# Token mixing in batches 2 to 4: one column half for each pair of TensorE column groups, and another order of the later steps

## The chip, the cores and the metric

The kernel runs on one core of a Trainium2 chip. Its time is the device time of one execution in microseconds, lower is better; several executions are taken, and their median counts. A core has five engines that run their own instruction lists side by side and wait for each other through semaphores: TensorE (PE in the profile; its weight loads are PEld), VectorE (DVE), ScalarE (ACT), GpSimd (POOL) and SyncE (SP), the last two mostly for issuing transfers here. TensorE is an array of 128 rows and 128 columns that can be cut into blocks, such as four of 64x64 or four column groups of 128x32. It writes to PSUM, eight banks of 512 float32 numbers in each of 128 partitions; VectorE and ScalarE move results to SBUF.

## What is computed

Four batches, 768 tokens, 8 heads of 48 (384 columns together). First a delta-rule recurrence for each head, then a mixer on its output:

```python
y[:, :, t] = np.einsum('bhd,bhde->bhe', q[:, :, t], state)
v_old = np.einsum('bhde,bhd->bhe', state, kt)
state = state + bt[:, :, :, None] * np.einsum('bhd,bhe->bhde', kt, vt - v_old)
...
xt = x.transpose(0, 2, 1)
h = xt @ U @ V
u = x + h.transpose(0, 2, 1)
ch = np.maximum(u @ w_ch1, 0.0) @ w_ch2
return (u + ch).astype(np.float32)
```

U is 768 x 32 and V is 32 x 768. The token mixing of one batch is therefore two small products: the first, U transposed times x, is a 32 x 384 matrix with a sum over all 768 tokens; the second, V transposed times that, is added to x.

## The kernel before

All is float32. The recurrence is worked in chunks of 64 tokens, twelve a batch, from Gram matrices (`products`, L461), triangular solves (VectorE's pairs at L530 and L532, `joins`, L591 to L640) and a chain of small matmuls from chunk to chunk (`recur`, L687 to L790: `outputs`, states, corrections). Its output lands in the tile X, one half of the tile for each of two batches in turn. The mixer of a batch starts when all twelve chunks stand in X, while the recurrence of the next batch goes on beside it.

The mixer of batch b goes over three tiles of 256 tokens (i = 0, 1, 2). For each, `front(b, i)` mixes the tokens and turns the result (L1198, or L229 and L233) so that channels lie on partitions; `wide(b, i)` does the two channel layers (`channels`, L1264, and in a crossed form on 64x64 blocks at L221; `narrow`, L1358 and also L221; the sum into X at L1304). The first tile of batch 1, the last tile of batch 3 and all of batch 4 go through forms of their own (L1088 to L1143, L1041, L997). The code counts batches from 0: b = 1, 2, 3 are batches 2, 3 and 4.

The lines that the change touches are the head of `front`:

- First product, `token_product` (L1060): X holds tokens in six blocks of 128 on the partitions. For each of the four column groups g of the array (128 rows x 32 columns) it multiplies a 128 x 32 block of U with a 128 x 384 block of X. Groups 0 and 2 go over the even token blocks, groups 1 and 3 over the odd ones, so groups 0 and 2 have one sum and groups 1 and 3 the other, each twice. Twelve matmuls of 384 columns a batch, into one PSUM bank.
- L1172 copies the result, 128 partitions x 384 columns, to the SBUF tile `tt`. Partitions 0 to 63 and 64 to 127 hold the same two partial sums.
- Second product (L1186), in each of the three tiles: the array is cut into four 64x64 blocks. A block's 64 rows are the even and the odd partial sum, which the product adds up; V lies on the partitions four times (`v_sb`). Block row m makes the m-th 128 tokens of the tile, block column q one half of these. Four matmuls of 384 columns; block row m writes to bank m of a pair.
- L1189 adds both banks to X, 128 x 768 numbers.

Nothing chooses an order at run time. Each part (`front`, `channels`, `recur`, a load and so on) is a generator that yields whenever it wants to put an instruction or a small group on an engine. `ORDER`, a written-out list of 2719 numbers, says whose turn it is; behind a point stands the PSUM bank pair, and a q chooses the crossed form of a step. An engine runs its own steps in the order of this list, and semaphores hold it where data or a buffer is not ready. Numbers are given to parts as they begin, so one number can mean another part when the list changes.

Of the kernel before, what the change touches and what calls it, by code (L numbers as in the profile page):

```python
# [11 lines left out]
ALU = mybir.AluOpType  # L12
# [11 lines left out]
def kernel(ctx: ExitStack, tc: tile.TileContext, q: bass.AP, k: bass.AP, v: bass.AP, beta: bass.AP, moe_U: bass.AP, moe_V: bass.AP, moe_w_ch1: bass.AP, moe_w_ch2: bass.AP, out: bass.AP):  # L24
# [59 lines left out]
    297 71 207 61 297 301 208 61 297 301 61 61 208 298.2 297 303 298 207 68 304q 208 298 70 71 304 44 207  # L84
# [6 lines left out]
    332 331 331 331 331 332.1 336 332 162 334.2 334 332 9.0 333 337q 334 9 206 328.2 9.0 337 9 9.0 337 328  # L91
    337 9 328 61 328 332 9.0 348.2 9 9.1 337 205 206 9 9.0 349 350.1 205 206 348 9 9.0 206 205 348 338q 348
    9 205 206 338 9.2 338 338 9 338 351.0 9.2 352 350 9 162 350 339q 350 9.2 339 9 351 339 9.1 80 89 90 89
# [3 lines left out]
    344q 353 9 353 364 9.2 353 344 353 85 360 9 365.1 344 9.2 360 344 360 9 78 78 364 9.0 344 9 78 364 9.2  # L97
    366.0 343 365 9 9.2 365 365 368 207 208 9 78 367 9.1 208 207 78 369.2 78 85 345q 207 208 208 207 345 85
# [3 lines left out]
    347 180 85 375 358 180.0 358 376 98 180 181.1 85 374.2 85 377q 98 181 104 377 388.0 104 85 377 85 375  # L102
# [6 lines left out]
    102 102 102 102 391 387 391 102 409 102 10.0 410 182q.2 10 102 10.0 394 411 10 394 182 102 102 411 102  # L109
    102 102 422.0 423 102 408.1 10.2 102 412q 10 102 10.2 102 422 412 10 422 102 10.2 422 102 424.0 10 412  # L110
    102 10.2 408 412 408 10 102 412 102 10.1 426.2 425 424 10 102 10.1 424 413q 102 424 10 102 10.0 102 413
# [7 lines left out]
    112 10 112 112 446.2 112 119 10.0 421 449 119 440 449 119 10 10.0 450 446 440 450 451q 446 10 446 119  # L119
    119 10.1 451 119 10 119 462.0 119 10.2 451 119 451 10 119 119 10.1 119 462 451 119 10 447.2 119 464 119  # L120
    10.1 119 112 452 10 119 119 447 447 452 119 119 119 463.1 465 10.2 119 453 119 462 462 119 119 10 453
    119 119 10.0 466 468.2 463 10 119 10.0 463 454q 463 119 10 467 10.1 119 454 211 212 10 119 10.0 454 468
    211 212 469.1 10 468 162 10.0 212 376 468 454 10 162 211 212 10.2 119 454 409 10 119 471.0 211 470 10.2
    119 469 119 455 119 119 119 455 119 10 119 456 119 472 119 469 119 469 456 119 119 119 10.2 119 473 119
    10 119 471 141 141 141 140 141 140 131 140 140 131 458q 471 132 471 132 183.1 474 467 119 119 131 458
    183 140 141 119 183.2 162 141 140 458 458 119 141 138 183 138 141 458 119 138 139 119 183q.0 119 140 139
# [4 lines left out]
    121 136 481.2 136 142 501 481 136 491 136 481 136 481 136 483 136 491 136 136 136 136 184q.0 136 136  # L131
# [1320 lines left out]
```

## Time and profile before

| | us |
|---|---|
| median of three runs | 573.75 |
| lowest, highest | 572.85, 576.26 |
| the profiled execution, its own time | 572.55 |
| span of its instructions on the core | 570.8 |
| mean granted TensorE clock over the span | 0.976 |
| first product, L1060, all four batches: passes, mean of one | 96, 0.490 |
| second product, L1186, all twelve tiles: passes, mean of one | 96, 0.500 |
| sum into X, L1189, all twelve tiles: count, mean of one | 12, 0.943 |

The span goes from the first instruction to the last; the profiled execution's own time has 1.75 us around it. A float32 matmul appears in the profile as two passes, each with a weight load of its own (PEld). Passes on different blocks of the array run at the same time, so the durations of passes cannot be added up; the chain of waits gives what a group of them costs from the start of one to the start of the next. The page divides the span into 40 slices of 14.3 us with the busy share of each engine in tenths.

### The profile page before, as it was taken

How to read it: one execution, taken by the hardware profiler on the slowest of the kernel's cores; microseconds unless marked ns; L12 is line 12 of the kernel's file. 1: busy time of each engine (PE TensorE's matmuls, PEld its weight loads, DVE VectorE, ACT ScalarE, POOL GpSimd, SP SyncE). 2: the span in 40 equal slices, each digit the busy share in tenths (PEclk: the TensorE clock that was granted, in tenths of full speed). 3: DMA queues.
4: the chain of work that ended last, by engine and by line, in shares of the span. 5: the costliest groups of instructions: out<-in, count | busy, mean ns of one | idle time of the engine just before them, and what ended most of it. 6: DMA issues, size and time to landing. Idle time of an engine off the chain costs nothing.

```text
span 570.8 us, 24657 instructions
## 1 busy us (share of the span) xinstructions
PE 537.4 (94%) x10965; PEld 454.7 (80%) x10965; DVE 417.4 (73%) x1062; ACT 243.1 (43%) x525; POOL 130.0 (23%) x229
## 2 busy tenths in 40 slices
PE   4776989999999999999999999999999999999997
PEld 4675877669789688789879977988879888656997
DVE  5798976799897439999887889999653356656542
ACT  3786885452435453155236433632452341336100
POOL 8061064552201453131044133400000000000000
PEclk9997579999999999999999999999999999999999
DMA  9957766542200353250033233310000000100001
GB/s 144 184 124 224 229 179 138 117 100 53 72 3 17 78 126 85 53 103 3 3 78 83 66 86 64 81 27 2 17 4 2 31 2 1 41 2 0 15 14 57
DMA packets 70763, 38.67 MB, mean 68 GB/s; under 512 B 56768, under 2 KB 67776, under 8 KB 70656
## 3 DMA queue, kind: packets, MB, share of 16 engines
q1 hardware_dynamic: 62368, 25.87, 19.2%
q0 software_dynamic: 6688, 10.92, 8.2%
q8 instruction: 86, 1.41, 1.1%
q10 hardware_dynamic: 1600, 0.30, 0.3%
q14 instruction: 21, 0.17, 0.1%
HBM read 32.34 MB, written 4.72 MB: 65 GB/s over the span
## 4 chain that ended last, share of the span: by engine, by line
PE 82%; DVE 8%; ACT 3%; DMA 2%; SPq 2%; issue 2%; DVEq 0%; ACTq 0%
PE P L1358 26%; PE P L1264 14%; PE P L221 9%; PE P L997 7%; PE P L461 4%; PE P L1041 2%; PE P L1088 2%; PE P L780 2%; PE P L739 2%; PE P L752 2%; DMA slot<-in_k_dram 2%; PE P L1186 2%; PE P L687 1%; PE P L1060 1%; PE P L694 1%
## 5 line engine op out<-in xcount | busy, mean ns | idle before, releaser
L1264 PE MATMUL P<-ut,w_sb 128*128 128x256 f32 x360 | 83.1, 385 | 0.2 <-ACT hs L1234 0.2
L1358 PE MATMUL P<-w_sb,hs 128*128 128x192 f32 x456 | 80.4, 330 | 0.0
L1358 PEld LDWEIGHTS P<-w_sb,hs 128*128 128x128 f32 x456 | 73.9, 190 | 3.9 <-issue 1.8
L1264 PEld LDWEIGHTS P<-ut,w_sb 128*128 128x128 f32 x360 | 66.7, 190 | 9.6 <-ACT hs L1234 0.3
L532 DVE TENSOR_TENSOR xt<-xt,prod 128x112 f32<-128x112 f32 (+21 forms) x200 | 64.2, 321 | 5.1
L530 DVE TENSOR_TENSOR prod<-gs,xt 128x112 f32<-128x112 f32 (+21 forms) x200 | 63.7, 318 | 4.3
L1304 DVE TENSOR_TENSOR X<-X,P 128x192 f32<-128x192 f32 x85 | 29.4, 347 | 42.9 <-PE P L1358 42.1
L344 POOL DMA_DIRECT2D slot<-in_k_dram x48 | 27.7, 582 | 95.5 <-PE P L780 60.9
L1234 ACT ACTIVATE hs<-P 128x512 f32<-128x512 f32 x42 | 24.9, 598 | 56.2 <-PE P L1264 43.6
L677 ACT COPY X<-P 64x192 f32<-64x192 f32 x96 | 30.1, 313 | 35.1 <-PE P L694 30.4
L1358 PE MATMUL P<-w_sb,S 128*128 128x192 f32 x240 | 41.3, 328 | 0.0
L1358 PEld LDWEIGHTS P<-w_sb,S 128*128 128x128 f32 x240 | 39.0, 190 | 0.8 <-DVE X L1304 0.6
L221 PE MATMUL P<-ut,w_sb 64*64 64x256 f32 x576 | 39.0, 383 | 0.2
L653 ACT COPY slot<-zz 32x384 f32<-32x384 f32 x64 | 34.5, 540 | 8.4 <-DVE zz L536 5.4
L461 PE MATMUL P<-slot 48*64 48x64 f32 x1536 | 33.1, 243 | 4.0 <-ACT slot L437 3.0
L461 PEld LDWEIGHTS P<-slot 48*64 48x64 f32 x1536 | 30.3, 156 | 7.4 <-ACT slot L437 3.6
L344 POOL DMA_DIRECT2D slot<-in_q_dram x48 | 27.2, 572 | 32.7 <-DVE slot L450 14.4
L657 POOL MEMSET slot<- 32x384 f32 x32 | 13.8, 431 | 90.9 <-PE P L628 89.8
L788 DVE TENSOR_TENSOR s<-s,P 128x192 f32<-128x192 f32 x40 | 14.0, 351 | 22.6 <-PE P L780 16.3
L982 DVE TENSOR_TENSOR slot<-slot,P 128x384 f32<-128x384 f32 x36 | 18.6, 551 | 15.8 <-PE P L997 15.5
L1358 PE MATMUL P<-w_sb,slot 128*128 128x192 f32 x180 | 29.9, 326 | 0.0
L1358 PEld LDWEIGHTS P<-w_sb,slot 128*128 128x128 f32 x180 | 29.4, 190 | 0.3
(205 smaller groups left out, 1059.1 us busy)
## 6 DMA issues: line engine op xcount, KB each, us to landing
w_sb<-in_moe_w_ch_dram SPq DMA_DIRECT2D x14, 384.0 KB, 5.2
out_dram<-X SPq DMA_DIRECT2D x22, 192.0 KB, 2.8
slot<-in_k_dram SPq DMA_DIRECT2D x36, 72.0 KB, 3.7
slot<-in_k_dram POOLq DMA_DIRECT2D x32, 72.0 KB, 3.3
slot<-in_v_dram SPq DMA_DIRECT2D x32, 72.0 KB, 3.0
slot<-in_v_dram POOLq DMA_DIRECT2D x32, 72.0 KB, 2.7
X<-in_moe_w_ch_dram SPq DMA_DIRECT2D x6, 384.0 KB, 4.6
wide<-in_moe_w_ch_dram SPq DMA_DIRECT2D x4, 384.0 KB, 5.8
```

The costliest lines, as they stand in the source:

```text
L221: nc.tensor.matmul(to[half(g)], w[half(r), half(g)], x[half(r)], start=start, stop=stop, skip_group_check=True)
L344: queue.dma_start(out=in_pairs(n, int(name == 'q'), j)[quarter(2 * par + y), :, g, 0:cols.stop - cols.start], in_=of[:, :, cols])
L461: nc.tensor.matmul(p_g[half(g ^ par * i), par, c], kq[rows, c, j, 0, half(g)], kq[rows, c, j, i, half(g)], start=True, stop=True)
L530: nc.vector.tensor_tensor(out=prod, in0=gb[:, :, j, j + 1:, None].to_broadcast([128, split, w, m]), in1=xb[:, :, j:j + 1, 0:m].to_broadcas ...
L532: nc.vector.tensor_tensor(out=xb[:, :, j + 1:, 0:m], in0=xb[:, :, j + 1:, 0:m], in1=prod, op=ALU.subtract)
L653: nc.scalar.copy(pg[quarter(i), :, at, :, a:a + BK], thirds(h)[quarter(i)].rearrange('p r (c j) t -> p r c j t', j=2))
L677: nc.scalar.copy(x[half(c % 2), c // 2, 4 * D * g:4 * D * (g + 1)].rearrange('p (j r d) -> p r j d', r=2, d=D), states(p_y)[half(g)])
L997: nc.tensor.matmul(banks[x], w1_sb[:, 4 * a[0] + e, a[1]] if isinstance(a, tuple) else w1_mixes[a][:, e], tokens(*t) if isinstance(t, tupl ...
L1234: nc.scalar.activation(hs[:, fs[0]:fs[1] + 1:fs[1] - fs[0]], p_f, ACTF.Relu)
L1264: nc.tensor.matmul(p_f[:, x], w(x, t), ut[:, t], start=t == 0, stop=t == KT - 1)
L1304: nc.vector.tensor_tensor(out=to, in0=to, in1=p, op=ALU.add)
L1358: nc.tensor.matmul(to, of[0], of[1], start=of[2], stop=of[3], skip_group_check=True)
```

## The change

The first batch keeps its form. In batches 2 to 4 the column groups g = 0, 1 take the first 192 columns of X and g = 2, 3 the other 192. The first product is still twelve matmuls, of 192 columns each. Partitions 0 to 63 of the result now hold the even and odd sums of the first 192 columns, partitions 64 to 127 those of the last 192. The copy to `tt` is 192 columns wide. The second product has to take both halves of the columns for both 128-token blocks: block row r does the columns 192 r to 192 r + 191 of every token block m, so there are eight matmuls of 192 columns in place of four of 384, and bank r of the pair holds column half r instead of token block m. The sum into X reads and writes X in the order (column half, token block, column) to match.

The second part is the list `ORDER`. Of its 2719 numbers 1638 differ at their place; in the first third these are a few neighbours that change places, from there on the order is another one. The steps are the same 2719. Of TensorE's 706 steps 235 stand at another place of its own list, by at most 14 places; of VectorE's 1042 there are 566, of ScalarE's 527 there are 216, of GpSimd's 218 there are 104 and of SyncE's 226 there are 94.

```diff
     ORDER = """
...
-    220 148 12 221.2 2 2 219 2 21 12 146 219 146 12 217 12 17.3 12 12 221 19 19 21 19 19 32.1 19 221 149 19
+    220 148 12 221.2 2 2 219 2 21 12 146 219 146 12 217 12 17.3 12 12 221 19 21 19 19 19 32.1 19 221 149 19
...
-    def token_product(p_t, x, ys):
+    def token_product(p_t, x, ys, split=False):
         for y in ys:
             for g in range(4):
                 c = 2 * y + g % 2
-                nc.tensor.matmul(p_t[R * g:R * g + R], u_sb[:, c], x[:, c], start=y == 0, stop=y == NB // 2 - 1)
+                cols = slice(HD * (g // 2), HD * (g // 2) + HD) if split else slice(0, DM)
+                nc.tensor.matmul(p_t[R * g:R * g + R], u_sb[:, c], x[:, c, cols], start=y == 0, stop=y == NB // 2 - 1)
...
             o = (yield op('pe', mode='T', take='pair'))
-            p_t = one(o)[:, 0:DM]
-            token_product(p_t, x, range(NB // 2))
+            p_t = one(o)[:, 0:HD]
+            token_product(p_t, x, range(NB // 2), True)
             yield op('dve')
-            nc.vector.tensor_copy(out=reserve_tt(b), in_=p_t)
+            nc.vector.tensor_copy(out=reserve_tt(b)[:, 0:HD], in_=p_t)
...
         p_h = pair(o)[:, :, 0:DM]
+        to = x[:, at]
+        if b > 0:
+            p_h, to = (p_h.rearrange('p r (m d) -> p r m d', m=NT), to.rearrange('p m (r d) -> p r m d', r=2))
         for q in range(2):
             for m, c in enumerate(cs):
-                nc.tensor.matmul(p_h[half(q), m], v_sb[half(m), c * 128 + L * q:][:, 0:L], tt[half(m)], start=True, stop=True)
+                if b == 0:
+                    nc.tensor.matmul(p_h[half(q), m], v_sb[half(m), c * 128 + L * q:][:, 0:L], tt[half(m)], start=True, stop=True)
+                    continue
+                for r in range(2):
+                    nc.tensor.matmul(p_h[half(q), r, m], v_sb[half(r), c * 128 + L * q:][:, 0:L], tt[half(r), 0:HD], start=True, stop=True)
...
-        nc.vector.tensor_tensor(out=x[:, at], in0=x[:, at], in1=p_h, op=ALU.add)
+        nc.vector.tensor_tensor(out=to, in0=to, in1=p_h, op=ALU.add)
```

Here HD is 192, DM 384, NT 2, R 32, L 64 and NB 6. Two places of the order by name. Around batch 2's first product, TensorE's list before was: first half of a second-layer product (L1358), two query-key products (L461), first product, second half of the L1358 product, second product; it is now: both halves of L1358, first product, the two query-key products, second product. In batch 3 the second product of the middle tile moves back, from behind the turning of the first tile to behind two more second-layer halves and half of a third.

More of the change, by code (lines that the diff above doesn't have):

```diff
@@ L81 @@
     283.0 51 176 289 58 51 58 279 290 276 283 51 277 283 64 283 64 279 283 51 70 71 291 277 53 71 276 51 70
[2 rows of a table removed]
-    297 71 207 61 297 301 208 61 297 301 61 61 208 298.2 297 303 298 207 68 304q 208 298 70 71 304 44 207
[1 row of a table removed]
[2 rows of a table added]
+    297 71 207 61 297 301 208 61 297 301 61 61 298.2 208 303 297 298 207 68 304q 298 208 70 71 304 44 207
[1 row of a table added]
     68 68 68 305 68 68 68 68 306 317 68 68 68 306 68 68 68 9.0 68 300.2 9 300 68 68 307 300 318 68 292 319
     307 68 68 68 9.0 68 300.2 68 9 321 300 319 284.1 319 300 302.0 300 300 299 68 299 308 68 299 68 299 308
[3 rows of a table removed]
@@ L91 @@
-    332 331 331 331 331 332.1 336 332 162 334.2 334 332 9.0 333 337q 334 9 206 328.2 9.0 337 9 9.0 337 328
-    337 9 328 61 328 332 9.0 348.2 9 9.1 337 205 206 9 9.0 349 350.1 205 206 348 9 9.0 206 205 348 338q 348
-    9 205 206 338 9.2 338 338 9 338 351.0 9.2 352 350 9 162 350 339q 350 9.2 339 9 351 339 9.1 80 89 90 89
[3 rows of a table removed]
-    344q 353 9 353 364 9.2 353 344 353 85 360 9 365.1 344 9.2 360 344 360 9 78 78 364 9.0 344 9 78 364 9.2
-    366.0 343 365 9 9.2 365 365 368 207 208 9 78 367 9.1 208 207 78 369.2 78 85 345q 207 208 208 207 345 85
[3 rows of a table removed]
@@ L102 @@
-    347 180 85 375 358 180.0 358 376 98 180 181.1 85 374.2 85 377q 98 181 104 377 388.0 104 85 377 85 375
[6 rows of a table removed]
-    102 102 102 102 391 387 391 102 409 102 10.0 410 182q.2 10 102 10.0 394 411 10 394 182 102 102 411 102
-    102 102 422.0 423 102 408.1 10.2 102 412q 10 102 10.2 102 422 412 10 422 102 10.2 422 102 424.0 10 412
-    102 10.2 408 412 408 10 102 412 102 10.1 426.2 425 424 10 102 10.1 424 413q 102 424 10 102 10.0 102 413
[7 rows of a table removed]
-    112 10 112 112 446.2 112 119 10.0 421 449 119 440 449 119 10 10.0 450 446 440 450 451q 446 10 446 119
@@ L120 @@
[L120 to L124, printed above, removed]
@@ L125 @@
-    10 119 471 141 141 141 140 141 140 131 140 140 131 458q 471 132 471 132 183.1 474 467 119 119 131 458
-    183 140 141 119 183.2 162 141 140 458 458 119 141 138 183 138 141 458 119 138 139 119 183q.0 119 140 139
[4 rows of a table removed]
-    121 136 481.2 136 142 501 481 136 491 136 481 136 481 136 483 136 491 136 136 136 136 184q.0 136 136
[3 rows of a table removed]
-    11.0 510 498q 136 11 496 510 11.0 498 136 11 136 11.2 136 514.0 498 513 136 498 136 513 513 11 136 11.1
-    136 498 11 136 136 11.2 136 185.1 11 136 515 11.2 136 185 514 11 499 516 514 136 514 136 136 136 136 136
@@ L137 @@
-    499 136 518 136 523 522 500 519 522 519 522 522 11.2 524 523.1 11 523 517.0 523 522 11.2 525q 522 11 525
-    536.1 11.2 525 525 11 521 520 11.2 525 11 517 11.2 537 536 214 213 213 213 520 526q 214 517 517 214 526
-    214 536 214 536 521.0 214 521 213 526 520 526 214 520 520 214 520 11 526 521 521.1 521 538 11.2 539.0
-    521 527q 11 521 11.2 527 11 11.1 527 527 11 11.2 527 11 540.1 214 11.2 213 541 539 214 539 528 214 539
-    214 542 542 528 542 529 543 11 529 530 544 530 532 545 532 547 546 546 546 533 531 548 533 549 11.0 550
@@ L142 @@
-    523.2 11 523 11.0 523 540 534q 11 523 540 540 11.0 534 11 551.2 11.1 534 534 11 11.0 534 11 213 11.1
-    552.0 554 11 554 11.1 551 11 551 553 11.1 551 552 555.2 11 552 552 11.1 11 11.0 535q 11 556.1 11.0 535
[13 rows of a table removed]
[3 rows of a table added]
+    333 332 331 331 331 331 332.1 336 332 162 334.2 336 334 332 9.0 333 334 337q 9 328.2 9.0 337 9 9.0 337
+    328 337 9 328 61 328 332 9.0 348.2 9 1 9.1 337 205 206 9 9.0 349 350.1 205 206 348 9 162 9.0 206 205 348
+    338q 348 162 9 205 206 338 333 9.2 338 9 338 338 351.0 9.2 352 350 9 339q 9.2 339 9 351 339 350 9.2 89
[3 rows of a table added]
@@ new lines @@
+    344q 364 354 9 354 364 9.1 354 344 9 354 85 9.1 360 344 365.0 9 357 78 9.1 344 360 78 9 360 78 78 9.2 78
+    365 78 344 9 365 85 365 366.1 9.2 368 9 367 9.0 345q 208 9 207 85 343 208 207 9.2 345 85 208 207 85 9 85
[3 rows of a table added]
+    374 361 347 109 104 180 109 104 358 108 358 85 180.2 108 85 104 85 180 181.1 85 375.0 378 101 379q 101
[6 rows of a table added]
+    102 408 102 102 389 102 102 102 102 102 182q.2 102 102 10.0 409 390.1 182 10 409 102 10.0 102 411 10 390
+    102 410 102 411 390 102 102 422.2 423 10.0 102 406.1 10 412q 406 102 406 102 10.0 102 412 10 424.1 102
@@ new lines @@
+    10.0 412 412 102 10 102 10.0 102 422 412 10 422 102 10.0 422 424 425 426.2 10 102 10.0 424 102 424 413q
[8 rows of a table added]
+    445 119 451q 10 445 119 445 119 10.2 119 451 119 10 462.0 119 10.2 451 451 10 119 444 10.2 119 462 451
+    10 119 447.1 119 464 119 10.2 119 452 10 119 462 462 119 119 463.2 119 10.0 119 452 119 119 10 453 447
+    465 119 119 453 119 119 447 10.0 119 466 463 468.1 10 463 119 10.0 463 454q 119 10 119 10.2 454 10 212
+    211 119 10.0 454 469.2 212 211 468 10 162 10.0 211 212 468 454 468 119 10 212 211 10.1 454 10 119 471.0
@@ new lines @@
+    470 467 10.1 119 455 119 119 119 455 467 119 119 456 467 472 10 119 456 119 119 119 119 469 473 10.1 119
+    119 10 458q 469 119 469 474 471 131 140 141 140 141 140 141 140 141 474 458 471 134 471 131 183.1 458
+    131 119 140 141 474 458 183 449 141 112 132 183.2 141 132 475.0 138 183 458 475 138 134 475 183q.1 143
[3 rows of a table added]
+    129 184 121 484 484 484 490 112 490 129 129 136 184q.1 501 136 136 489 488.0 136 184 489 136 162 483.2
[3 rows of a table added]
+    497 11 509 185 136 11.0 136 511 497 11 136 504 136 136 11.2 512 510 513.0 11 510 504 11.2 510 498q 136
@@ new lines @@
+    11 136 136 11.1 498 11 496 11.2 514.1 498 136 513 498 11 513 136 513 136 11.2 136 498 11 136 136 11.0
+    136 185.2 11 515 11.0 185 514 11 499 516 514 136 514 136 136 136 136 499 136 136 136 136 136 136 518 136
+    500 129 523 522 162 522 523.0 522 519 523 524 519 517.2 522 521 522 11.1 525q 523 522 524 11 520 11.0
+    525 11 536.1 525 11.0 520 525 11 520 129 11.0 525 11 517 11.0 537 536 214 213 517 526q 214 520 214 11
+    536 214 526 536 213 521.0 521 213 526 526 520 521 517 213 520 526 139 213 521.1 521 538 214 11.0 214 214
@@ L157 @@
+    521 527q 11 521 11.2 527 11 539.0 11.1 527 527 11 11.2 527 11 540.1 214 11.2 541 539 539 542 528 539 213
+    542 528 542 213 529 543 529 530 544 11 530 532 545 532 547 546 546 546 11.0 531 523.2 533 11 548 533 549
+    523 550 11.0 523 534q 11 523 214 214 11.0 540 551.2 11 540 11.0 540 534 11 11.1 552.0 534 551 11 11.1
+    551 534 551 11 11.2 534 11 11.1 552 553 555.2 11 552 554 552 11.1 214 554 535q 11 11.0 535 11 565.1 11.0
[13 rows of a table added]
     """
```

122 rows, old and new, of the table ORDER are left out of this document.

## The prediction

> **What bounds the kernel now.** I read the head of the page first, then the slices, then the chain of waits in short.
>
> ```profile
> span 570.8 us, 24657 instructions
> PE 537.4 (94%) x10965; PEld 454.7 (80%) x10965; DVE 417.4 (73%) x1062; ACT 243.1 (43%) x525; POOL 130.0 (23%) x229
> ...
> PE   4776989999999999999999999999999999999997
> ...
> DVE  5798976799897439999887889999653356656542
> ...
> PEclk9997579999999999999999999999999999999999
> ...
> PE 82%; DVE 8%; ACT 3%; DMA 2%; SPq 2%; issue 2%; DVEq 0%; ACTq 0%
> ```
>
> The reader is to see that TensorE is busy at 9 tenths or more from the ninth slice to the last but one, at the full granted clock from the seventh on, and that 82% of the chain that ended last is TensorE's. So a microsecond of TensorE work taken out of this stretch should come off the span, unless VectorE, also at 9 in several slices, is then late. Next I asked for busy time by stages, from about where the order of the steps begins to differ (175 us) to the end of the last front (488 us), and for what TensorE waited for there.
>
> ```profile
> 230.00:290.00 60.00, 59.39 (x1159) 49.47 (x1156) 53.98 (x140) 22.32 (x50) 11.62 (x20) 1.00 0.19 41
> 345.00:390.00 45.00, 44.48 (x888) 36.91 (x886) 41.59 (x104) 18.83 (x39) 11.30 (x19) 1.00 0.24 53
> sum 313.00, PE 308.08 PEld 263.50 DVE 229.48 ACT 123.03 POOL 66.31; mean PE 51.35 PEld 43.92 DVE 38.25 ACT 20.50 POOL 11.05
> ...
> PE P L780 <- ACT z L755: 1.0, 3, 0.5
> PE P L694 <- ACT z L755: 0.8, 2, 0.5
> PE P L739 <- DVE rec L402: 0.7, 1, 0.7
> PE P L739 <- DVE s L788: 0.6, 3, 0.3
> PE P L687 <- DVE s L788: 0.4, 2, 0.2
> ```
>
> The columns are length, then PE, PEld, DVE, ACT and POOL; the sum is over six stages. TensorE idles 313.00 - 308.08 = 4.9 us in all, of which the five waits shown are 3.5, the longest 0.7, none of them on a DMA. A new order has at most 4.9 us of idle time to win here. VectorE idles 6.0 us in the stage that holds batch 2's first product and 3.4 us in the stage of batch 3's.
>
> **The first product.** The chain in order of time gives its three places, and the rows by shape give what stands around it.
>
> ```profile
> 230.08 2.07 PE P L1060 x24
> 232.15 2.15 PE P L1358 x12
> 234.30 0.81 PE P L1186 x8
> ...
> 347.94 2.07 PE P L1060 x24
> 350.01 1.14 PE P L221 x24
> 351.15 0.65 PE P L1186 x8
> ...
> 466.86 2.07 PE P L1060 x24
> ...
> 166.28 1.95 PE P L1358 x12
> ```
>
> L1060 is 12 matmuls of 384 columns a batch; each float32 matmul is two passes, so x24. They stand on the chain with all of their 2.07 us in each of the three batches that change. How they run is seen in two short windows of the timeline:
>
> ```profile
> 230.01 0.53 PE L1060 MATMUL P<-X,u_sb 128*32 128x384 f32 x4
> 230.01 0.85 PE L1060 MATMUL P<-X,u_sb 128*32 128x384 f32 x8
> ```
>
> By 230.06 four passes had started, by 230.4 eight: the four column groups (128x32 blocks of the array) run side by side, in rounds of four. Six rounds cost 2.07 us. A round of 384 columns is 0.65 / 2 = 0.325 us, from the x8 of L1186 between neighbours on the same block size (two rounds). A pass of 192 columns is 1.95 / 12 = 0.1625 us, from L1358, which runs one pass at a time. So a round lasts as long as its columns, 0.85 ns each, and halving them saves 6 x (0.325 - 0.1625) = 0.975 us a batch, **2.9 us** for three. The number of matmuls and of weight loads stays. If something fixed per round stood below the columns, the saving would be smaller; nothing in these two rows shows one, so I keep 2.5 as the lower end.
>
> **The copy to tt** (L1172) goes from 384 to 192 columns.
>
> ```profile
> 232.38 0.55 DVE L1172 COPY tt<-P 128x384 f32<-128x384 f32 x1
> L1304 DVE TENSOR_TENSOR X<-X,P 128x192 f32<-128x192 f32 x85 | 29.4, 347 | 42.9 <-PE P L1358 42.1 <-PE P L221 0.6
> L1189 DVE TENSOR_TENSOR X<-X,P 128x768 f32<-128x768 f32 x12 | 11.3, 943 | 3.0 <-PE P L1186 3.0
> ```
>
> By the nearest row of that width it takes 0.35 us, 0.2 less, on VectorE. I cost it at nothing: in batch 2 the copy ran 232.38 to 232.93, inside the 2.15 us of L1358 that lie between first and second product. Were that cover gone, the copy would be on the path, and shorter than before. In the new order batch 2 has two query-key products (L461) there; batch 3 has half of a crossed second-layer product (L221 x24, as at 350.01), batch 4 the second-layer half that was there. All are longer than the copy. The sum into X (L1189) has the same 768 elements and another order of them, 943 ns; VectorE reads rows of 192 from the same two banks, and I keep 943. Twice the 384-column row (1.10) would be +0.16 us each, nine times, on VectorE only.
>
> **The second product** is the open price. Before: four matmuls of 384 columns, one on each 64x64 block. After: eight of 192, in the order row 0, row 1, row 0, row 1 of column group 0, then the same of group 1. It is done in nine fronts (three in each of batches 2 to 4). If the four blocks still run side by side, its 16 passes are four rounds of 0.1625 = 0.65 us, as now: price 0. But the first eight passes in the list lie on two blocks only. If the array cannot reach past them, it runs two at a time: eight rounds, 1.30 us, +0.65 us a front, 5.9 us in all. The rows on this:
>
> ```profile
> 118.48 1.06 PE P L1135 x8
> ...
> 62.97 0.25 PE L591 MATMUL P<-zz,hs 64*64 64x16 f32 x1
> 62.98 0.31 PE L780 MATMUL P<-z,slot 64*48 64x48 f32 x3
> 63.06 0.26 PE L591 MATMUL P<-zz,hs 64*64 64x16 f32 x2
> 63.09 0.28 PE L780 MATMUL P<-z,slot 64*48 64x48 f32 x2
> ```
>
> L1135 has two blocks in turn and 256 columns: at 0.85 ns a column four rounds of two are 0.87 us, and with a change of block size (0.2, below) the 1.06 of the row, so passes on one block never overlap. The other four rows are a timeline: in the list of instructions as built, all of this L780 stands ahead of the L591 that starts at 62.97, and yet five passes of L780 start after it. So the array does start a pass on a free block over five earlier ones that wait for theirs. The second product needs six (the waiting passes of the first two blocks are 2 x 3), and seven for the fourth block. If five were the limit, the third and fourth block would start one round late: five rounds, +0.16 us, nine times, 1.5 us. I take 0, because six and seven are near five and the same row pattern (four passes at once where the two passes of one matmul stand side by side in the list) occurs everywhere. The ends for the range are 0 and +5.9.
>
> The Trainium skill, page "TensorE: Matmul & The Clock Gate", section "Part 3: Packing small matmuls — row/col tiling", says that matmuls start and end strictly in program order and only weight loads are pulled ahead. The trace disagrees in the strict form: the L780 rows above start behind a later L591. If the rule did hold, the second product would have each pass wait for the one ahead in the list, and the price would lie on the side of the rival below.
>
> **The new order.** TensorE has the same steps before and after; 235 of 706 stand elsewhere in its list, by at most 14 places, the first of them behind the second half of the last tile of batch 1. In the list as built, the block size of the array changes 170 times before and 166 after. A change costs 2.15 - 1.95 = 0.20 us by L1358 and 0.81 - 0.65 = 0.16 by L1186: 4 x 0.18 = **0.7 us** less. No step gets a new kind of wait. Moved steps that others wait for are VectorE's scalings of v and block transposes (up to 71 places) and loads on POOL's and SP's queues (up to 27 and 26 places), where K, V and Q blocks of batches 3 and 4 pass one another. TensorE waited for none of these from 175 us on; a load in the way costs its landing,
>
> ```profile
> slot<-in_q_dram POOLq DMA_DIRECT2D x24, 60.0 KB, 3.1
> ```
>
> 3.1 us at worst where nothing covers it. Taken: 0 beyond the block changes, since the stalls left are small and spread; ends -2.5 (half of the 4.9 us of idle time) and +3.1.
>
> **Sum**: -2.9 - 0.7 + 0 = -3.6 us. On the profiled execution (572.55, its span 570.8 and 1.75 around it) that is 568.95; the median of the three runs stands 1.2 above that execution, so the forecast is 573.75 - 3.6 = **570.2 us**.
>
> **Rivals.** *The second product runs two blocks at a time* (slower): +5.9 - 3.6 = +2.3, **576.0 us**. For it: the order in the list, and no row that reaches past six. Against: the five that are shown, and the fours of L1060. It decides from a price of 3.6 / 9 = 0.40 us a front; with one late round (+0.16) the time would be 571.7 and still below before. By the skill's strict order the rounds per front would be nine, since only neighbours in the list could overlap: 9 x 0.1625 - 0.65 = 0.81 us, 577.4 us; I give that form 3%, inside this rival's 18%.
>
> *VectorE becomes the bound of the two stages*: TensorE is done earlier and waits for it. Then only batch 4's 0.975 and the block changes count: -1.7, **572.1 us**. For it: 90% and 92% of VectorE in those stages. Against: it idles 6.0 and 3.4 us there and gets 0.2 us of work less. 15%.
>
> *The new order removes stalls too*: half of the idle time goes, -3.6 - 2.5, **567.7 us**. For it: the waits are all for ACT and VectorE steps that moved. Against: the ones shown are eleven, none over 0.7. 15%.
>
> *The new order makes a stall*: one load or scaling late by 3.1, **573.3 us**, or several. 10%. That the change does not do what it says has no room: the list as built has the 192-column matmuls.
>
> **Numbers.** The forecast keeps 42%. 1% (5.7 us) is about what a measurement of this kernel can tell from no change. Faster by over 1% (below 568.0) needs nearly all of the third rival, 14%; slower by over 1% (above 579.5) needs the first rival and a new stall together, 5%; within 1% is the rest, 81%. The range takes in the forecast, both late-VectorE and one-late-round cases, the gain side to 567.0 and the first rival's 576.0.
>
> **What would show it.** In the changed kernel's chain L1061 x24 should read about 1.1 us in place of 2.07, and the second product (L1194, x16) 0.65 to 0.81. If it reads 1.3 or more, or if a short window at its start shows two passes and not four, the first rival holds. The copy should read 0.35. TensorE's idle time between 175 us and the last front should stay under 5 us; more, with waits on VectorE in the two stages, speaks for the second rival, a wait on a load for the fourth. The forecast is wrong if the saving is seen in L1061 and not in the span.

## The result, and the profile after

The changed kernel takes 570.18 us (median of 9 runs, 568.11 to 571.82), the kernel before 573.68 (9 runs beside it, 572.83 to 576.42). The ratio on record is **0.9917, 95% interval 0.9891 to 0.9942**: a gain of 0.6 to 1.1%. It is not the quotient of the two medians, which is 0.9939 and lies inside the interval. Its profiled execution took 569.18 us, 3.4 less than that of before. The forecast was 570.2.

The head of the page, the slices and the shares of the chain of waits, changed kernel:

```profile
span 567.5 us, 24793 instructions
...
PE 534.2 (94%) x11037; PEld 458.5 (81%) x11037; DVE 417.8 (74%) x1062; ACT 242.8 (43%) x525; POOL 129.5 (23%) x229
...
PE   4676889899999999999999999999999999999997
...
PE 82%; DVE 8%; ACT 4%; DMA 2%; issue 2%; SPq 1%; DVEq 0%; ACTq 0%
```

The picture is the one of before: TensorE at 9 tenths, 82% of the chain, 3.2 us less busy, with 72 more passes (9 fronts, 8 more each). The chain in order of time at batch 2 and at batch 3 (start, length, what; the two second products behind L461 and L233 belong to the first two tiles of batch 2):

```profile
231.78 1.11 PE P L1061 x24
232.89 1.56 PE P L461 x96
234.45 0.70 PE P L1194 x15
235.15 2.15 PE P L1366 x12
237.30 0.52 PE P L233 x11
237.82 0.82 PE P L1194 x16
...
348.39 1.11 PE P L1061 x24
349.50 1.14 PE P L221 x24
350.64 0.69 PE P L1194 x15
```

The first product fell from 2.07 to 1.11 us in each of the three batches (batch 4 has the same row). The second product reads 0.69 to 0.83 in all nine fronts, 7.01 us in all against 6.82 before. That its four blocks run at once is seen in a window of 50 ns at its start (the second row; count at the end):

```profile
237.53 0.29 PE L233 MATMUL P<-ident,X 64*128 64x64 f32 x4
237.75 0.41 PE L1194 MATMUL P<-tt,v_sb 64*64 64x192 f32 x4
```

The copy and the sum into X by line (count, then min/median/max in ns):

```profile
L1173 DVE COPY tt<-P x3: 320/344/350, 233.4 to 469.0; 128x192 f32<-128x192 f32 x3
...
L1197 DVE TENSOR_TENSOR X<-X,P x12: 941/947/955, 116.4 to 478.3; 128x768 f32<-128x768 f32 x12
```

Where the time went is not so plain. The whole span mixes the changed part with a part that is the same in both kernels and doesn't repeat well: from the start of the first batch's first layer to batch 1's first product, some 77 to 107 us, the traces of all kernels take from 30.5 to 36.9 us. So from here on I use the **changed stretch**: from batch 2's first product to the start of the last tile's first layer (L997), read from the starts of their passes. It took 257.59 us before and 252.60 now. Busy time in its three stages, first of the kernel before, then of the changed one (length, then PE, PEld, DVE, ACT, POOL, granted clock, DMA share, GB/s):

```profile
230.01:347.87 117.86, 116.02 (x2418) 97.55 (x2412) 101.63 (x265) 47.44 (x109) 30.27 (x53) 1.00 0.25 58
347.87:466.79 118.92, 117.55 (x2500) 103.37 (x2496) 79.11 (x199) 44.97 (x103) 12.95 (x23) 1.00 0.11 27
466.79:487.60 20.81, 20.81 (x152) 16.99 (x152) 15.01 (x28) 4.27 (x7) 0.00 (x0) 1.00 0.00 1
sum 257.59, PE 254.38 PEld 217.91 DVE 195.74 ACT 96.67 POOL 43.22; mean PE 84.79 PEld 72.64 DVE 65.25 ACT 32.22 POOL 14.41
```

```profile
231.71:348.32 116.61, 114.82 (x2546) 98.97 (x2545) 101.80 (x267) 47.34 (x108) 34.03 (x60) 1.00 0.25 58
348.32:464.41 116.09, 115.44 (x2500) 104.08 (x2497) 77.94 (x195) 44.52 (x102) 11.70 (x21) 1.00 0.12 31
464.41:484.31 19.90, 19.90 (x176) 18.00 (x176) 15.54 (x29) 4.58 (x7) 0.00 (x0) 1.00 0.03 10
sum 252.60, PE 250.16 PEld 221.05 DVE 195.28 ACT 96.45 POOL 45.73; mean PE 83.39 PEld 73.68 DVE 65.09 ACT 32.15 POOL 15.24
```

The clock is 1.00 throughout. The stretch lost 5.0 us, not the 3.6 of the forecast: 4.2 of TensorE's busy time and 0.8 of its idle time. In the profiled execution 1.7 us of that is hidden by a later start of the stretch (231.71 against 230.01). Five microseconds against 3.6 is what the experiments had to explain.

### The profile page after: what moved, and what is told of

Read it like the earlier page. It is cut to its first block, busy times and chain, and to the rows that moved or that the text cites. A ratio compares the mean times of both kernels' runs of the same rounds, so it can differ in the third digit from the quotient of the medians.

```text
span 567.5 us, 24793 instructions
## 1 busy us (share of the span) xinstructions
PE 534.2 (94%) x11037; PEld 458.5 (81%) x11037; DVE 417.8 (74%) x1062; ACT 242.8 (43%) x525; POOL 129.5 (23%) x229
## 3 DMA queue, kind: packets, MB, share of 16 engines
q8 instruction: 86, 1.41, 1.1%
## 4 chain that ended last, share of the span: by engine, by line
PE 82%; DVE 8%; ACT 4%; DMA 2%; issue 2%; SPq 1%; DVEq 0%; ACTq 0%
PE P L1366 25%; PE P L1272 14%; PE P L221 9%; PE P L997 7%; PE P L461 4%; PE P L1041 2%; PE P L1089 2%; PE P L780 2%; PE P L752 2%; PE P L739 2%; PE P L687 2%; PE P L694 1%; DMA slot<-in_k_dram 1%; PE P L1194 1%; DMA w_sb<-in_moe_w_ch_dram 1%
## 5 line engine op out<-in xcount | busy, mean ns | idle before, releaser
L1272 PE MATMUL P<-ut,w_sb 128*128 128x256 f32 x360 | 81.9, 383 | 0.2 <-ACT hs L1242 0.2
L1366 PE MATMUL P<-w_sb,hs 128*128 128x192 f32 x456 | 80.4, 330 | 0.0
L1366 PEld LDWEIGHTS P<-w_sb,hs 128*128 128x128 f32 x456 | 73.9, 190 | 1.8 <-issue 0.9
L1366 PE MATMUL P<-w_sb,S 128*128 128x192 f32 x240 | 42.0, 329 | 0.0
L221 PE MATMUL P<-ut,w_sb 64*64 64x256 f32 x576 | 39.5, 383 | 0.4 <-DVE X L1312 0.2
L1366 PEld LDWEIGHTS P<-w_sb,S 128*128 128x128 f32 x240 | 39.0, 190 | 0.8 <-issue 0.6
L461 PE MATMUL P<-slot 48*64 48x64 f32 x1536 | 33.7, 243 | 4.5 <-ACT slot L437 2.9
L461 PEld LDWEIGHTS P<-slot 48*64 48x64 f32 x1536 | 30.7, 156 | 7.1 <-ACT slot L437 3.5
L1366 PE MATMUL P<-w_sb,slot 128*128 128x192 f32 x180 | 29.9, 326 | 0.0
L1366 PEld LDWEIGHTS P<-w_sb,slot 128*128 128x128 f32 x180 | 29.4, 190 | 0.3
```

Source lines behind the costliest of these rows:

```text
L221: nc.tensor.matmul(to[half(g)], w[half(r), half(g)], x[half(r)], start=start, stop=stop, skip_group_check=True)
L461: nc.tensor.matmul(p_g[half(g ^ par * i), par, c], kq[rows, c, j, 0, half(g)], kq[rows, c, j, i, half(g)], start=True, stop=True)
L1272: nc.tensor.matmul(p_f[:, x], w(x, t), ut[:, t], start=t == 0, stop=t == KT - 1)
L1366: nc.tensor.matmul(to, of[0], of[1], start=of[2], stop=of[3], skip_group_check=True)
```

## The experiments

**Is the stretch a fair measure?** Both kernels as they are, on another occasion.

> The changed kernel once more, as the measure for the runs beside it. Theory A (the two products bring most of the gain): about 3.5 us under the kernel before, ratio near 0.994. Theory B (the order brings as much as the products or more): 4.5 to 5 us, ratio near 0.992, as the interval of the first comparison has it.

> The kernel before, once more, for a second trace. From the start of batch 2's first product to the end of batch 4's last front and first-layer start (the stretch that took 257.6 us in the first trace of it, 252.6 in both traces of the changed kernel) it should again take 257 to 258 us, if single stalls do not make the difference. Ratio 1.

The changed kernel again: 569.5 us median, ratio 0.9918 [0.9885, 0.9951]; its stretch 252.62. Before again: ratio 1.0015 [0.9980, 1.0049], its stretch 258.43, 0.4 more than was expected. The changed kernel repeats within 0.02 us, and the ratio is the same to a ten-thousandth, while the piece from 77 to 107 us took 5 us more in both of these traces. The stretch can tell what the span cannot. The two traces of before differ in it by 0.8 us, so smaller differences need more than the stretch.

**Each part alone.** First the new products under the old list, then the old products under the new one.

```diff
 # products_old_order: against the changed kernel
-    ORDER = (the list of the changed kernel)
+    ORDER = (the list of the kernel before)
 # order_old_products: against the kernel before
-    ORDER = (the list of the kernel before)
+    ORDER = (the list of the changed kernel)
```

> The new products under the list of steps of the kernel before. Both theories: L1061 x24 at 1.11 us in batches 2 to 4, saving 3 x 0.96 = 2.9 us, and the nine second products up to 0.2 us dearer together: -2.7 us, ratio 0.995. If the old list leaves a wait where TensorE is now early, less than that (above 0.997).

> The old products under the new list of steps. Theory A: four changes of block size fewer and nothing else, -0.7 us, ratio 0.999. Theory B: stalls go as well, -2 us or more, ratio 0.9965 or lower. A ratio over 1 would say that the new list pays only with the shorter products.

> The new products under the old list, once more. In its first trace the stretch took 257.7 us, as before the change: 0.97 was won at batch 2's first product, and 1.2 lost at 314 us in a stall of TensorE inside a run of L1366 that waits for nothing the profile shows; 0.85 won at batch 3's, and lost again at the copy to tt (0.4) and at 420 us (0.7). If the stall at 314 is chance, the stretch takes about 256.4 now; if the old list cannot use the time (theory B), 257.5 again.

> The old products under the new list, once more: the stretch at 256.5 us as in its first trace (1.1 under before) by theory A and B alike; 255.5 or less if its first trace had a chance stall too, which would give the order 2 us by itself.

Products alone: ratios 0.9978 [0.9943, 1.0014] and, again, 0.9955 [0.9918, 0.9992]. Order alone: 0.9966 [0.9926, 1.0006] and 0.9960 [0.9926, 0.9994]. The stretches say more: products alone 257.71 and 257.70, so nothing gained against the first trace of before (257.59); order alone 256.49 and 255.78, 1.1 and 1.8 gained; both 5.0. By its expectation the second 257.70 would say that the old list cannot use the time; the stops below give another reason. The sums over the three stages, products alone and then order alone:

```profile
sum 257.71, PE 252.79 PEld 221.51 DVE 194.86 ACT 96.72 POOL 43.16; mean PE 84.26 PEld 73.84 DVE 64.95 ACT 32.24 POOL 14.39
```

```profile
sum 256.49, PE 253.26 PEld 218.02 DVE 196.24 ACT 96.60 POOL 45.72; mean PE 84.42 PEld 72.67 DVE 65.41 ACT 32.20 POOL 15.24
```

Products alone has 1.6 us less busy time than before and 4.9 us of idle time in place of 3.2. What TensorE waited for in this stretch, first trace (in all, times, longest, us):

```profile
PE P L1366 <- issue: 1.0, 1, 1.0
...
PE P L1194 <- DVE tt L1173: 0.4, 2, 0.2
PE P L221 <- issue: 0.3, 1, 0.3
```

Two kinds of rows are there that neither before nor after has. The second product waits for the copy to tt, in two of three batches. And "issue": TensorE stands still in the middle of a run of matmuls of one line, and no semaphore explains it, as the chain shows:

```profile
312.66 1.50 PE P L1366 x8
314.16 1.04 issue
315.20 1.89 PE P L1366 x10
```

**The wait for the copy.** In batch 3 the first product ended at 349.41 in the second trace of products alone, and VectorE had other work ahead of the copy in its list:

```profile
349.26 0.33 DVE L530 TENSOR_TENSOR prod<-gs,xt 128x175 f32<-128x175 f32 x1
349.63 0.34 DVE L532 TENSOR_TENSOR xt<-xt,prod 128x175 f32<-128x175 f32 x1
349.89 0.57 DVE L450 STREAM_TRANSPOSE slot<-slot 128x384 f32<-128x384 f32 x1
350.38 0.32 DVE L1173 COPY tt<-P 128x192 f32<-128x192 f32 x1
```

The experiment moves the copy up in batches 3 and 4:

```diff
 # products_copy_first: against products_old_order, tokens of ORDER
-    119 119 131 458 183        (183: batch 3's copy)
+    183 119 119 131 458
-    560 562 560 186            (186: batch 4's copy)
+    186 560 562 560
```

> Products alone, with the copy to tt moved up in VectorE's list: in batch 3 ahead of a multiply, a subtract and a block transpose, in batch 4 ahead of two sums over the hidden layer. In products alone two of the three second products waited for this copy, 0.4 us in all on TensorE and 1.0 us on its weight loads. If this queue is where products alone loses its lead, the row that shows TensorE waiting for tt is gone, and the stretch from batch 2's first product to the last tile's first layer falls by 0.4 to 0.9 us from 257.7, to 256.8 to 257.3. If the copy only takes the place of what was late behind it, the stretch stays 257.7 +- 0.2 us, with a new wait on VectorE at the places of the solves and sums that the copy passed.

The stretch was 257.01, within what was expected for a late copy, and the row of the wait for tt is gone. The second product now starts 2.14 us behind the start of the first in batch 3 (2.53 in products_again) and 3.26 in batch 4 (3.48): 0.6 us won at the two places. In batch 4, which has nothing else in the way, the stage shows it: 19.90 us, as in the changed kernel, against 20.13. In batch 3 the rest of the stage differs from trace to trace by more than the 0.4. On the whole run nothing can be seen (ratio 1.0010 [0.9966, 1.0053]). In the changed kernel's own trace nobody waits for the copy; its start of the second product in batch 3 is 2.14 too.

**The stops without a semaphore.** The page of every run has a queue that brings in instructions; in the changed kernel it is

```profile
q8 instruction: 86, 1.41, 1.1%
```

86 packets of 16 KB. TensorE's list has 22,174 entries in this trace, a load and a matmul for each of the 11,037 passes and 100 of its sequencer. The 1.41 MB are 63.5 bytes for each of them; with 64 bytes an entry, an estimate from these two numbers, a packet is a piece of 256 entries. I counted, for each stop, how many entries of the list stand ahead of the pass behind it. In the two traces of products alone the stops stood at 47.77, 56.77, 75.77, 78.77 and 79.77 pieces (56.77 and 75.77 in both): always 0.77 of a piece. That could be chance of this list, so the next two kernels push the list along by half a piece. In front of batch 1's first product they put 32 small matmuls whose results are overwritten:

```diff
 # products_shifted (against products_old_order), new_shifted (against the changed kernel)
+            for n in range(8):
+                for g in range(4):
+                    nc.tensor.matmul(p_t[R * g:R * g + R, 0:16], u_sb[:, g], x[:, g, 0:16], start=True, stop=True)
             token_product(p_t, x, (0, 1))
```

> Products alone (the new products under the list ORDER of before), with 32 small matmuls (16 columns each, results overwritten at once) put ahead of batch 1's first product. They add 128 instructions to TensorE's list, half of one 16 KB piece in which the list is brought into the core; nothing else changes. In both traces of products alone, TensorE stood still without a semaphore for 0.2 to 1.0 us at the same three places of its list (47.77, 56.77 and 75.77 pieces from its head). Theory A, supply of instructions: the places belong to the list's pieces, so the work that stood there now runs without a stop (L1366 84 us behind the first product of batch 2, L221 at 190 us behind it), and stops, if any, stand half a piece away; the stretch from batch 2's first product to the last tile's first layer changes, to anything from 256.0 to 258.5 us. Theory B, the stops belong to the work (a wait that the trace does not show): the same matmuls stop again and the stretch is 257.7 +- 0.2 us as before.

> The changed kernel with the same 128 extra TensorE instructions ahead of batch 1's first product. Theory A: the changed kernel's lead of 5 us in this stretch is partly luck of where its pieces fall, so the stretch from batch 2's first product to the last tile's first layer is longer than 252.6 us by one or two stops of 0.3 to 1.0 us, 253 to 254.5 us. Theory B: 252.6 +- 0.2 us as in both traces of the changed kernel.

Products, shifted: stretch 258.31, ratio 1.0108 [0.9977, 1.0240], which settles nothing by itself. Changed kernel, shifted: stretch **257.64 in place of 252.60**, ratio 1.0054 [1.0005, 1.0104]. So the changed kernel with about one microsecond of extra matmuls is slower than before. Part of that lies ahead of the stretch, where it has five more stops, the longest of 1.7 us. Waits of the shifted changed kernel in the stretch:

```profile
PE P L639 <- issue: 1.2, 1, 1.2
PE P L640 <- issue: 0.9, 1, 0.9
PE P L687 <- issue: 0.7, 1, 0.7
PE P L461 <- DVE slot L450: 0.6, 1, 0.6
PE P L694 <- issue: 0.5, 1, 0.5
```

Four of the five first rows are stops; the changed kernel has the one on L450 and none of the others. Of the five places at which products alone had stopped, four ran through once the list was shifted. At the fifth (79.77) the passes wait 0.3 us for VectorE in any case, so that stop had cost nothing. Other passes stopped instead, again at 0.77 of a piece, as in the middle of this run of small blocks in the shifted products (timeline: start, length, line, tile and block, count, idle time ahead):

```profile
268.41 0.19 PE L640 MATMUL P<-zz 32*32 32x32 f32 x1
269.92 0.18 PE L639 MATMUL P<-zz 32*32 32x32 f32 x1 [1.31 <-issue]
```

The place, counted from the two lists and the DMA records, with the packet that landed last before it:

```
kernel              stopped until   entry / 256   stood still   packet started, landed
products_old_order     315.20          56.77         1.04          312.68   313.56
products_again         420.63          75.77         0.23          417.80   419.18
products_shifted       164.75          29.77         1.68          162.16   163.49
products_shifted       269.92          47.77         1.31          267.21   268.38
new_shifted            384.01          67.77         1.21          381.69   382.65
new_shifted            434.62          76.77         0.70          431.78   433.19
```

In thirteen traces the timeline has 33 stops on "issue" of 0.2 us or more from 110 to 500 us. All 33 stand at 0.76 to 0.78 of a piece, in shifted and unshifted lists alike. The fourteenth, second_block_by_block's, has three more at the same place. (Counted by the records of the traces alone, which hold some five entries fewer than the built lists, all 36 stand at 0.75 to 0.76.) At the stops of the table TensorE went on 1.3 to 1.6 us after a packet had landed and 2.3 to 2.9 after it had started. The same holds where it did not stop: at 868 such places from 110 to 500 us in the fourteen traces no pass started less than 1.19 us after its packet had landed. So theory A holds, and theory B fell: these stops belong to the supply of the instruction list, not to the work. Only the size in the changed kernel was off, 257.6 where 253 to 254.5 was expected. Most of the larger ones stand among short passes on small blocks (L461, L639, L640). Where a place stops in one trace and not in its twin, its packet came later: at 56.77 it began 2.12 us after TensorE had passed 55.77 in products_old_order, which then stood still for 1.04, and 1.01 us after it in products_again, which stood still for 0.16. Why a packet begins late is open, and whether the order of other transfers has a part in it was not tried.

The stretch can now be read with the stops of 0.25 us or more taken out (the distance to the pass behind the boundary, less the usual distance of passes there; the one that a wait covers is left in):

```
                        stretch    stops    rest
before                   257.6      0.3     257.3
before again             258.4      0.6     257.8
products alone           257.7      1.9     255.8
  again                  257.7      1.7     256.0
  shifted                258.3      2.8     255.6
order alone              256.5      1.2     255.3
  again                  255.8      0.6     255.2
both (changed kernel)    252.6      0       252.6
  again                  252.6      0       252.6
  shifted                257.6      4.7     253.0
```

The rest is steady to 0.5 us within each kind; a wait that a stop covers may make it up to 0.3 too low. Against the mean of before, 257.6, products alone win 1.8, order alone 2.3, both 4.6 to 5.0. So the two parts nearly add up once the stops are out. The 0.5 to 0.9 left over may be the 0.6 that products alone lose to the wait for the copy, which the new list does not have. This is not shown: products_copy_first, which is not in the table, has 1.3 to 1.5 of stops in its 257.0 and a rest of 255.5 to 255.7, only 0.1 to 0.3 below products alone, and the rest varies by 0.5.

**The second product.** Three other orders for the same columns; in the last, pieces of 96.

```diff
 # the changed kernel: for q: for m: for r      (neighbours in the list on two blocks)
 # second_in_turn: four neighbours on four blocks
+        for m, q, r in [(m, q, r) for m in range(2) for q in range(2) for r in range(2)]:
 # second_block_by_block: 4 passes for a block, then the next
+        for q, r, m in [(q, r, m) for q in range(2) for r in range(2) for m in range(2)]:
 # second_in_pieces: 8 passes of 96 columns for a block, then the next
+        for q, r, m, z in [(q, r, m, z) for q in range(2) for r in range(2) for m in range(2) for z in range(2)]:
```

> The changed kernel with the second product's eight matmuls in another order: token block outermost, then column group, then block row, so that four matmuls that follow one another lie on four blocks. If the array reaches past all passes that wait on a busy block, as the starts 26 ns apart in the changed kernel's trace suggest, the nine second products get at most 0.02 to 0.03 us shorter each: 0.2 us, not to be told from the changed kernel (ratio to it 0.9995). If reach is short in some places and costs a round (0.16), up to 1.5 us faster.

> The changed kernel with the second product's matmuls sorted by block: both of block 1, both of block 2, then 3, then 4. The last block's first pass stands behind 12 passes in the list, 9 of which wait. If the array reaches that far, L1194 x16 stays at 0.69 to 0.85 us on the chain and all four blocks start within 0.1 us of each other; ratio to the changed kernel 1. If reach ends at the six or seven that the changed kernel needed, one or two rounds more (0.16 to 0.33 us), nine times: 1.5 to 3 us slower.

> The changed kernel with the second product cut into pieces of 96 columns, block after block: eight passes for one 64x64 block in a row in the list, then eight for the next, 32 passes a front in place of 16, with the same columns in all. If the array reaches past any number of waiting passes, the four blocks start together and a front takes 0.65 to 0.85 us as now. If the reach ends, at some count between the 9 passes that it is known to pass and the 21 that the fourth block needs here, the last block or two start late: a front takes up to twice as long, 1.0 to 1.3 us, and a short window at its start shows two or three blocks in place of four.

In turn: ratio 0.9923 [0.9887, 0.9958], stretch 253.5, 252.6 without stops; its nine second products read 6.83 us on the chain in place of 7.01, the 0.2 that was expected. Block by block: 0.9926 [0.9897, 0.9955], stretch 254.0, nine fronts 7.07. On the whole run neither can be told from the changed kernel. Block by block, the list has twelve passes of three blocks ahead of the first one of the fourth, nine of them waiting, and yet the chain has

```profile
477.54 0.83 PE P L1195 x16
```

and the four blocks started within 0.04 us of each other. In pieces: ratio 1.0177 [1.0109, 1.0246], stretch 265.1. The chain at one of its fronts, and then a window of the timeline from 480.80 to 481.20:

```profile
480.86 1.96 PE P L1196 x32
```

```profile
480.79 0.68 PE L1196 MATMUL P<-tt,v_sb 64*64 64x96 f32 x6
```

1.96 us for the columns that took 0.82, more than the 1.0 to 1.3 that were expected, and in 0.4 us only six passes had started; by their distances five of them are one block's. The first pass of the second block started 0.39 us behind the first of the first block, between the fifth and the sixth pass of that block; the third and fourth followed at 0.77 and 1.16. So a later block starts here as soon as no more than three passes of the block ahead are waiting. Four passes a block in a row leave three waiting, and nothing is lost, whatever the sum over the blocks is (nine at most in these kernels); eight leave seven, and each block is 0.39 late. Five to seven in a row were not tried. That the limit is by block, and not a total, follows from nine waiting passes being reached past in one kernel and seven not in the other.

## Why the prediction was right, point by point

**The time** was right, 570.2 for 570.18, but that it fits to 0.02 us is luck. One of its terms, the new order, was too small, and the sum with it: -3.6 against -5.0 in the stretch (2.9 - 0.2 + 2.3). The whole-run ratio says -4.8 us [-6.3, -3.3] of 573.68, which holds both; the two medians are 3.5 apart. In the profiled execution the rest went to the unrepeatable piece ahead of the stretch.

**The first product** was right: 2.07 to 1.11, 0.96 for 0.975 a batch, 2.9 us. What six rounds cost beyond their columns stayed as it was (2.07 - 1.95 = 0.12 us before, 1.11 - 0.975 = 0.135 after), so the saving was that of the columns.

**The second product at price 0** was right in its mechanism: +0.19 us over nine fronts, not 5.9, and not even the 1.5 of one late round. The reason given, that six and seven are near five, was weaker than the fact. By the later runs it is not the sum of the waiting passes that counts but how many of them are for one block, and three is the most here. The first rival fell. So did the strict order of the Trainium skill (page "TensorE: Matmul & The Clock Gate", section "Part 3: Packing small matmuls — row/col tiling"): by it the front would take nine rounds, 1.46 us; it took 0.82, with passes starting ahead of nine earlier ones. second_in_pieces shows a limit, but one that the page does not state either.

**The copy at nothing** was right in the changed kernel (0.34 us, and nobody waits for it) and wrong with the old list, where the shorter first product and a full VectorE list left it 0.6 us late. The cover was there in all three batches with the old list too (L1366, the old L1358, 2.15 us in batches 2 and 4, L221 with 1.14 in batch 3). In two of them it was not enough, because VectorE came to the copy too late: the prediction weighed the cover against the length of the copy and did not ask what stands ahead of the copy on VectorE. The second rival (VectorE becomes the bound) is true to this size for products alone; the copy moved up removes the wait, and so does the new list.

**The new order** is the term that was mis-sized: 0.7 predicted, 2.3 measured alone (stops taken out). Of these, about 1.0 is waiting: TensorE's waits on other engines in the stretch add up to 2.7 us in both traces of before and to 1.7 in both of order alone. The block changes are 0.7 by the prediction's working. The 0.6 left has no name: TensorE's busy time falls by 1.1 between the first traces (254.38 to 253.26), but it differs by 0.7 between the two traces of before (254.38, 255.09). The longest waits of the kernel before in the stretch:

```profile
PE P L694 <- ACT z L755: 0.8, 2, 0.5
PE P L780 <- ACT z L755: 0.7, 2, 0.5
PE P L739 <- DVE s L788: 0.6, 3, 0.3
```

With the new list L694 has no such row, L780 has one wait of 0.2, L739 has 0.3 in all (order alone) or 0.2 (changed kernel); one of 0.6 on L450 is new. So the third rival, a new order that removes stalls too, was nearer than the forecast for this term: 0.7 + 2.5 = 3.2 by the rival, 0.7 by the forecast, 2.3 measured. The prediction gave it 15%; for a list that moves 235 steps it ought to have had as much as no gain at all. The fourth rival fell: no wait on a load.

**TensorE's idle time** stayed under 5 us (2.4 in the stretch), and VectorE is not late, as "what would show it" asked. What no step of the prediction reckoned with is the instruction list. The stops that it makes take nothing in the changed kernel's stretch and up to 4.7 us in the shifted one's, as much as the whole change, and they turned the sum of two parts into an apparent interaction.

## What to carry to other kernels

Halving the columns of matmuls that run side by side paid by the column here, and splitting them cost next to nothing with up to four passes of one block in a row; eight in a row more than doubled the time, so interleave the blocks. Before two parts of a change are called dependent on each other, look for idle time without a semaphore, and count where it stands in the engine's instruction list: 128 harmless instructions ahead moved these stops and made a kernel that gained 0.8% lose 0.5%. When a producer gets shorter, read the list of the engine that takes its result, not only the work beside the consumer.

## What the runs showed of the hardware that was not expected

- TensorE's list comes in packets of 16 KB, and it can stop for 0.2 to 1.7 us where a piece is not there in time: 33 stops of 33 at 0.77 of a piece, and at no place a pass less than 1.19 us after its packet had landed.
- Passes of different blocks start out of list order past nine waiting passes, but only past three of one block: 0.82 us a front with four passes a block in a row, 1.96 with eight of half the width.
- The piece from 77 us to batch 1's first product differs by 5 us between traces of one kernel, and with it goes the landing of one load. In the first trace of before VectorE's block transposes at this place run without a wait, in the second they wait for a Q block (timeline):

```profile
86.35 1.04 DVE L450 STREAM_TRANSPOSE slot<-slot 128x384 f32<-128x384 f32 x2
```

```profile
91.18 1.04 DVE L450 STREAM_TRANSPOSE slot<-slot 128x384 f32<-128x384 f32 x2 [4.16 <-DMA slot<-in_q_dram]
```

Four of the fourteen traces have this wait with 4.1 to 4.4 us and take 35.3 to 36.9 us for the piece; two have it with 1.9 and 3.2 us and take 32.2 and 33.9; the eight without it take 30.5 to 32.2. The granted clock does not sort them: it was 0.95 in this piece both in products_shifted (30.9 us) and in second_in_turn (35.8). What makes the load late was not tried.
